# Mixing keys and queries ahead of values in the prologue of a Sinkhorn attention and SwiGLU kernel

## The chip, the cores and the metric

The kernel runs on one core of a Trainium2 chip. The metric is the device time of one execution in microseconds (us), and the figure of the kernel is the median of its runs. A core has TensorE (PE) for matmuls, VectorE (DVE), ScalarE (ACT), GpSimd (POOL) and SyncE (SP), each with its own queue of instructions, worked off in order. Matmuls write to PSUM, everything else here lives in SBUF, and data comes from HBM by DMA. DMAs are issued from GpSimd's queue (all loads but one) and from SyncE's (the small sort_net load and all stores).

## The reference

The inputs are q, k and v with 4 batches, 8 heads, 768 positions and 64 features, a sort_net of 8x8 for each batch and head, and the three weights of a gated feed-forward layer with 512 inputs and 1536 hidden columns. Cut to what matters:

```python
P = sort_net
for _ in range(5):                       # Sinkhorn
    P = exp(P - max(P, -1))
    P = P / (sum(P, -1) + 1e-9)
    P = P / (sum(P, -2) + 1e-9)
k_sorted = einsum('bhij,bhjcd->bhicd', P, k_blocks)   # 8 blocks of 96 positions
v_sorted = einsum('bhij,bhjcd->bhicd', P, v_blocks)
scores = (q_blocks @ k_sorted_blocks.T) / sqrt(64)    # inside a block of 96
attn = softmax(scores)
x = (attn @ v_sorted_blocks)             # to 3072 tokens x 512
g = x @ w_gate
out = (g * sigmoid(g) * (x @ w_val)) @ w_out
```

So P mixes the blocks of keys and of values; the queries are not mixed, but the kernel sends them through the same matmuls to have them transposed.

## The kernel before

**Two stages.** A prologue makes the attention of the first half of batch 0 (units 0 to 3; a unit is two heads and four blocks). After it the feed-forward part runs over eight token groups of 384, n = 0 to 7: gate, value and output matmuls, into which the rest of the attention is merged (units, kqs, v_chunk). The function merge writes that order out from fixed costs, and the change leaves it alone.

**The order is written by hand.** In the prologue, manual_schedule covers PE, Pool, DVE and Activation: each engine takes its instructions in the order of the program text. From line 434 it covers PE and Pool alone.

**Loads.** GpSimd's queue holds, in order: values of batch 0 in two halves (L98), the identity matrix, queries and keys of batch 0 in halves (L92, L89), the first gate and value weights (L101), two copies that turn a quarter of the values each from position-major into feature-major (copy_v, L114, into vch), the other gate and value weights, batch 1's keys, queries and values, and the output weights (L138).

**Sinkhorn.** P is 32 rows (batch and head) by 64, in PSUM (p_ps). Each of five iterations is an exp on ScalarE (L174) and six VectorE instructions (L182 to L188; the last iteration ends with two products into p_bf at L191). Among them the kernel puts other work: in iteration 2, ahead of the reductions, VectorE makes mask (a 0/1 mask of heads, L177) and copies a part of the identity into rmix[0] (L178), and ScalarE copies eighths of the values into vch (L112) in iterations 2 and 3 and after the loop.

**Weights of the mixing.** At L357 sixteen small matmuls with p_bf spread P over the partitions (w_ps), once for partitions 0 to 63 and once for 64 to 127. mix_of(b) multiplies it by mask on VectorE, which gives vmix (values, L364) and rmix (keys and queries, L368). The identity part of rmix carries the queries through.

**Mixing batch 0.** Four chunks of values (L380: 16 matmuls each into a PSUM tile tv, drained into vt) come first, then six chunks of keys and queries (L390: 32 matmuls each into tkq, drained into kqt). Drains go to ScalarE and VectorE in turn (function drain: L201 and L199). Chunks 0 to 2 of tkq read the first half of the positions, 3 to 5 the second.

**The first four units.** For each unit qk_wide makes eight score matmuls (L405) and one exp over both heads (L410). av makes eight matmuls with the mixed values (L276) and normalises on VectorE (L280, L282, tile st). xtr transposes st (L296) and drains it into xt, which the gate matmuls read. fill(n) issues n matmuls on 512 columns whose results nobody reads (L348), as the ten warm matmuls ahead of the weights do.

**PSUM.** In the prologue, one pool of four buffers (pair_tile) serves all of this: p_ps, warm_ps, w_ps, tv, tkq, qk, av_ps and x_ps. A buffer comes free when its last reader is done.

Of the kernel before, what the change touches and what calls it, by code (L numbers as in the profile page):

```python
# [12 lines left out]
ALU = mybir.AluOpType  # L13
# [4 lines left out]
def kernel(  # L18
# [11 lines left out]
    nc = tc.nc  # L30

    B, H, S, D = q.shape
    NB = sort_net.shape[-1]
    C = S // NB
    BH = B * H
    H2 = H // 2
# [7 lines left out]
    R = H * NB  # L44
# [29 lines left out]
    vch = const.tile([128, D * C + 32], BF16)  # L74
# [5 lines left out]
    kq_tiles = {}  # L80
# [26 lines left out]
    def copy_v(eng, pair, rows, s, n=4):  # L107
        cs = slice(s * (C // n), (s + 1) * (C // n))
        dst = vch3[rows, :, cs]
        src = v_tiles[pair][rows, cs, :]  # L110
        if eng is nc.scalar:
            eng.copy(dst, src.transpose([0, 2, 1]))  # L112
        else:
            eng.tensor_copy(dst, src.transpose([0, 2, 1]))  # L114

    ident = const.tile([128, 128], BF16)
    lowr, highr = slice(0, R), slice(R, 2 * R)
# [22 lines left out]
    rmix = [const.tile([128, 2, 2, H2, NB], BF16, name=f"rmix{b}") for b in range(B)]  # L140
# [8 lines left out]
    def vt_tile(pair):  # L149
        if pair not in vts:  # L150
            t = vtp.tile([C, 2, H * NB, D + 1], BF16, name=f"vt{pair}", tag="vt")
            nc.vector.memset(t[:, :, :, D:D + 1].rearrange("p u n e -> p (u n) e"), 1.0)
            vts[pair] = t
        return vts[pair]
# [14 lines left out]
    def pair_tile(name):  # L169
        return psum.tile([128, 1024], FP32, name=name, tag="pair")  # L170

    p_ps = pair_tile("p_ps")[0:BH, 0:NB * NB].rearrange("p (i j) -> p i j", j=NB)
    for it in range(N_ITER):
        nc.scalar.activation(p_ps, p_sb if it == 0 else p_ps, AF.Exp)  # L174
        if it == 2:
            with nc.allow_low_precision("0/1 mask"):
                nc.vector.tensor_reduce(mask, id4, axis=AX.XY, op=ALU.add)  # L177
            nc.vector.tensor_copy(rmix[0][R:2 * R, :, 1, :, :], idq)  # L178
            copy_v(nc.scalar, 0, lowr, 2, 8)
        if it == 3:  # L180
            copy_v(nc.scalar, 0, lowr, 3, 8)
        nc.vector.reduce_sum(rowred[:, :, 0], p_ps, axis=AX.X)  # L182
        nc.vector.reciprocal(rowred, rowred)
        nc.vector.tensor_mul(p_ps, p_ps, rowred.to_broadcast([BH, NB, NB]))
        nc.vector.reduce_sum(colred[:, 0, :], p_ps.transpose([0, 2, 1]), axis=AX.X)
        nc.vector.reciprocal(colred, colred)
        if it < N_ITER - 1:
            nc.vector.tensor_mul(p_ps, p_ps, colred.to_broadcast([BH, NB, NB]))  # L188
# [8 lines left out]
    def drain(eng, dst, src):  # L197
        if eng == "v":
            nc.vector.tensor_copy(dst, src)  # L199
        else:  # L200
            nc.scalar.copy(dst, src)  # L201
# [3 lines left out]
    def kqt_tile(b):  # L205
        if b not in kqts:
            kqts[b] = kqp.tile([128, 2 * H2 * NB * C], BF16, name=f"kqt{b}", tag="kqt")
        return kqts[b]

    GI = H2 * NB  # L210
# [57 lines left out]
    def av(b, u, tag="av"):  # L268
        half, g = divmod(u, H2)
        vt = vts[b // 2][:, b % 2].rearrange("p (h i) e -> p h i e", h=H)  # L270
        av_ps = psum.tile([128, 2, 512], FP32, name="av_ps", tag=tag, bufs=4 if tag == "pair" else 1)
        o = av_ps[:, :, 0:4 * (D + 1)].rearrange("p two (i e) -> p two i e", e=D + 1)
        for two in range(2):
            e = es[(b, u)][two]
            for i4 in range(4):
                nc.tensor.matmul(o[:, two, i4, :], lhsT=e[:, i4 * C:i4 * C + 128],  # L276
                                 rhs=vt[:, 2 * g + two, half * 4 + i4, :],
                                 start=True, stop=True)
        r_sb = ssp.tile([C, 2, 4, 1], FP32, name="r_sb", tag="r")
        nc.vector.reciprocal(r_sb, o[0:C, :, :, D:D + 1])  # L280
        st = ssp.tile([C, 4, 2, D], BF16, name="st", tag="st")
        nc.vector.tensor_tensor(st.rearrange("p i two d -> p two i d"), o[0:C, :, :, 0:D],  # L282
                                r_sb.to_broadcast([C, 2, 4, D]), op=ALU.mult)
        sts[(b, u)] = st

    def xtr(b, u, eng, tag="att"):
        half, g = divmod(u, H2)
        if g == 0:
            xts[(b, half)] = xtp.tile([128, H2, TW], BF16, name=f"xt{b}_{half}", tag="xt")
        st = sts.pop((b, u))  # L290
        if tag == "pair":
            x_ps = pair_tile("x_ps").bitcast(BF16)[:, 0:4 * C].rearrange("p (a c) -> p a c", c=C)
        else:
            x_ps = psum.tile([128, 4, C], BF16, name="x_ps", tag=tag)
        for i4 in range(4):
            nc.tensor.transpose(x_ps[:, i4, :], st[:, i4].rearrange("p a b -> p (a b)"),  # L296
                                ident[0:C, 0:C])
        drain(eng, xts[(b, half)][:, g, :], x_ps.rearrange("p a b -> p (a b)"))
# [52 lines left out]
    warm(warm_ps[:, 0:128], lowr, v_tiles[0][lowr, HC:HC + 2, :].rearrange("p c d -> p (c d)"), 1)  # L351
    warm(warm_ps[:, 512:1024], slice(0, 128), warm_sb, 9)

    w_ps = pair_tile("w_ps")[:, 0:NB * B * H].rearrange("p (i b h) -> p i b h", b=B, h=H)
    for i in range(NB):
        for half in range(2):
            nc.tensor.matmul(w_ps[half * R:(half + 1) * R, i].rearrange("p b h -> p (b h)"),  # L357
                             lhsT=p_bf[:, i].rearrange("p a b -> p (a b)"),
                             rhs=ident[0:BH, 0:BH], start=True, stop=True)

    def mix_of(b):
        mk = mask[0:R].rearrange("p (g two) -> p two g", two=2)
        lo = (b % 2) * R
        nc.vector.tensor_tensor(  # L364
            vmix[b // 2][lo:lo + R, b % 2],
            mask[lo:lo + R].unsqueeze(2).to_broadcast([R, H, NB]),
            w_ps[lo:lo + R, :, b].transpose([0, 2, 1]), op=ALU.mult)
        nc.vector.tensor_tensor(  # L368
            rmix[b][0:R, :, 0],
            mk.unsqueeze(3).to_broadcast([R, 2, H2, NB]),  # L370
            w_ps[0:R, :, b].rearrange("p i (g two) -> p two g i", two=2), op=ALU.mult)

    mix_of(0)
    dst = vt_tile(0)[:, 0]
    mix = vmix[0][lowr, 0].rearrange("p a b -> p (a b)")
    for db in range(4):
        tp = pair_tile("tv").rearrange("p (l n) -> p l n", n=H * NB)
        for ld in range(16):
            at = (db * 16 + ld) * C
            nc.tensor.matmul(tp[:, ld, :], lhsT=vch[lowr, at:at + 128], rhs=mix,  # L380
                             start=True, stop=True)
        drain("sv"[db % 2], dst[:, :, ts(db, 16)], tp[0:C].transpose([0, 2, 1]))

    dst = kqt_tile(0).rearrange("p (n c) -> p n c", c=C)
    rm = rmix[0].rearrange("p two a g i -> p two (a g i)")
    for cb in range(6):
        tp = pair_tile("tkq").rearrange("p (l n) -> p l n", n=2 * GI)
        for lc in range(16):
            for two in range(2):
                nc.tensor.matmul(tp[two * D:(two + 1) * D, lc, :],  # L390
                                 lhsT=kq_tiles[0][:, cb * 16 + lc, :],
                                 rhs=rm[:, two, :], start=True, stop=True)
        drain("sv"[cb % 2], dst[:, :, ts(cb, 16)], tp.transpose([0, 2, 1]))
    for b in range(1, B):
        mix_of(b)

    def qk_wide(u):
        half, g = divmod(u, H2)
        flat = kqts[0]
        ps = pair_tile("qk").rearrange("p (two n) -> p two n", two=2)  # L400
        for i4 in range(4):
            at = (g * NB + half * 4 + i4) * C
            for two in range(2):
                lo = two * D
                nc.tensor.matmul(ps[:, two, i4 * C:(i4 + 1) * C], lhsT=flat[lo:lo + D, at:at + 128],  # L405
                                 rhs=flat[lo:lo + D, GI * C + at:GI * C + at + C],
                                 start=True, stop=True)
        n = ecount[0] % 8
        ecount[0] += 2
        nc.scalar.activation(e_all[:, n:n + 2, 0:4 * C], ps[0:C, :, 0:4 * C], AF.Exp, scale=scale)  # L410
        es[(0, u)] = [e_all[:, n, :], e_all[:, n + 1, :]]

    def fill(n):
        warm(pair_tile("warm_ps")[:, 0:512], slice(0, 128), kqts[0][:, 0:512], n)

    for u in range(4):
        qk_wide(u)
        fill(2)
        if u >= 1:
            av(0, u - 1, "pair")  # L420
            fill(1)
        if u >= 2:
            xtr(0, u - 2, "v", "pair")
    av(0, 3, "pair")
    xtr(0, 2, "s", "pair")
    fill(3)
    xtr(0, 3, "s", "pair")
    fill(2)
    for b in range(1, B):
# [105 lines left out]
```

## Time and profile before

| | |
|---|---|
| Runs of the kernel before | 279.53, 280.14, 281.66 us; median 280.14 |
| The profiled execution | 279.53 us, of which the span of the profile is 277.5 |
| TensorE busy | 253.9 us, 92% of the span, 2698 matmuls |
| VectorE busy | 170.6 us, 61%, 364 instructions |
| ScalarE busy | 124.3 us, 45%, 239 instructions |
| GpSimd busy | 46.5 us, 17%, 44 instructions |
| First value chunk, L380 | starts at 18.42 us |
| First key/query chunk, L390 | starts at 21.91 |
| First scores, L405 | start at 29.73 |
| First attention product, L276 | starts at 32.34 |
| First gate matmul, L310 | starts at 38.97 |

All times of the profile count from the start of its span. The rows of the profile name the line, the engine and the operation, then the tile written and the tiles read, with partitions x elements. A time behind "idle before" is what the engine waited, and the name behind the arrow is what ended the wait. PE is the matmul itself and PEld the load of its weights, which overlaps. The chain of waits is followed back from the last instruction, at each step to what released it.

In forty equal slices, the first six of the profile (41.6 us) hold the prologue; the rest is the feed-forward part with the attention of the other units in it.

### The profile page before, as it was taken

The numbers are of one execution on the slowest core, as the hardware profiler recorded it, in microseconds if no ns is written. First come the engines' busy times: TensorE is split into PE (matmuls) and PEld (weight loads), VectorE is DVE, ScalarE is ACT, GpSimd is POOL, SyncE is SP. The second block draws the span as 40 slices with busy tenths as digits, with TensorE's granted clock in tenths as the row PEclk, the third lists the DMA queues.
The fourth block names the chain that finished last, engine by engine and source line by source line (L and its number), as shares of the span: only waits on it lengthen the run. The fifth ranks groups of instructions, "written<-read, shape, count | busy, mean of one in ns | idle before, by whom it ended". The sixth has DMA issues, their size and how long they took to land.

```text
span 277.5 us, 6356 instructions
## 1 busy us (share of the span) xinstructions
PE 253.9 (92%) x2698; PEld 146.7 (53%) x2698; DVE 170.6 (61%) x364; ACT 124.3 (45%) x239; POOL 46.5 (17%) x44
## 2 busy tenths in 40 slices
PE   0647799999999899999999999999999999999994
PEld 0147445565556456556656456555555555555541
DVE  6956468787276587574267587574567566666500
ACT  3174454445563353437975353435342533223311
POOL 8964005930096000000000000000000000000000
PEclk9965799999999999999999999999999999999998
DMA  6999999189961000001101101001101111011121
GB/s 111 211 191 197 220 209 200 33 162 204 223 138 40 38 4 38 18 24 38 40 0 41 38 2 40 22 20 40 38 2 38 38 40 38 2 39 38 41 76 76
DMA packets 12620, 20.86 MB, mean 75 GB/s; under 512 B 880, under 2 KB 8560, under 8 KB 12016
## 3 DMA queue, kind: packets, MB, share of 16 engines
q0 software_dynamic: 9088, 14.16, 28.7%
q1 hardware_dynamic: 3504, 6.30, 6.0%
q8 instruction: 21, 0.34, 0.5%
q14 instruction: 7, 0.06, 0.1%
HBM read 28.32 MB, written 6.29 MB: 125 GB/s over the span
## 4 chain that ended last, share of the span: by engine, by line
PE 84%; DVE 10%; ACT 3%; issue 2%; ACTq 0%
PE o_ps L337 23%; PE v_ps L323 22%; PE g_ps L310 21%; PE tkq L219 4%; PE qk L256 3%; PE av_ps L276 2%; DVE rmix L178 2%; DVE st L282 2%; PE x_ps L296 2%; PE tkq L390 2%; DVE h L325 1%; PE warm_ps L348 1%; PE tv L241 1%; PE tv L380 1%; DVE gs_sb L315 1%
## 5 line engine op out<-in xcount | busy, mean ns | idle before, releaser
L315 DVE SCALAR_TENSOR_TENSOR gs_sb<-th_sb,g_ps 128x384 bf16<-128x384 bf16 x96 | 53.0, 552 | 61.9 <-ACT th_sb L313 60.3
L310 PE MATMUL g_ps<-xt,wg_sb 128*128 128x384 bf16 x384 | 78.3, 326 | 0.1
L323 PE MATMUL v_ps<-xt,wv_sb 128*128 128x384 bf16 x384 | 78.4, 326 | 0.0
L313 ACT ACTIVATE th_sb<-g_ps 128x384 bf16<-128x384 f32 x96 | 47.5, 495 | 56.6 <-PE g_ps L310 55.7
L337 PE MATMUL o_ps<-wo_sb,h 128*128 128x512 bf16 x288 | 68.6, 379 | 0.0
L325 DVE SCALAR_TENSOR_TENSOR h<-v_ps,gs_sb 128x384 bf16<-128x384 f32 x96 | 53.3, 555 | 7.6 <-PE tkq L219 0.5
L310 PEld LDWEIGHTS <-wg_sb 128*128 128x128 bf16 x384 | 34.5, 97 | 22.2 <-issue 0.6
L323 PEld LDWEIGHTS <-wv_sb 128*128 128x128 bf16 x384 | 33.9, 97 | 20.1
L337 PEld LDWEIGHTS <-h 128*128 128x128 bf16 x288 | 26.5, 98 | 27.5
L342 ACT COPY o_sb<-o_ps 128x512 f32<-128x512 f32 x24 | 14.1, 586 | 54.4 <-PE o_ps L337 54.3
L114 POOL COPY vch<-v 64x1536 bf16<-64x1536 bf16 (+1 forms) x10 | 28.1, 2860 | 29.7 <-DMA v<-in_v_dram 16.4
L263 ACT ACTIVATE e_all<-qk 96x384 bf16<-96x384 f32 x56 | 24.3, 488 | 5.6 <-PE qk L256 5.6
L201 ACT CAST vt<-tv 96x512 bf16<-96x512 f32 (+1 forms) x26 | 19.7, 788 | 6.2 <-PE tv L231 3.4
L282 DVE TENSOR_TENSOR st<-av_ps,r_sb 96x512 bf16<-96x512 f32 x32 | 21.9, 683 | 0.7
L199 DVE CAST kqt<-tkq 128x512 bf16<-128x512 f32 (+1 forms) x21 | 16.0, 761 | 5.8 <-PE tkq L219 3.2
L201 ACT CAST kqt<-tkq 128x512 bf16<-128x512 f32 (+1 forms) x21 | 13.5, 643 | 10.8 <-PE tkq L219 7.2
L276 PEld LDWEIGHTS <-e_all 96*128 96x128 bf16 x256 | 12.3, 99 | 6.9 <-issue 1.4
L276 PE MATMUL av_ps<-vt,e_all 96*128 96x65 bf16 x256 | 13.7, 195 | 0.7 <-DVE st L282 0.5
L219 PEld LDWEIGHTS <-kq 128*64 128x64 bf16 x576 | 10.5, 112 | 5.9 <-issue 5.9
L296 PE MATMUL x_ps<-ident,st 96*128 96x96 bf16 x128 | 10.8, 206 | 2.2 <-DVE st L282 2.1
L296 PEld LDWEIGHTS <-st 96*128 96x128 bf16 x128 | 8.5, 97 | 8.0 <-DVE st L282 4.0
L219 PE MATMUL tkq<-rmix,kq 128*64 128x64 bf16 x576 | 12.5, 197 | 0.0
(57 smaller groups left out, 132.4 us busy)
## 6 DMA issues: line engine op xcount, KB each, us to landing
out_dram<-o_sb SPq DMA_DIRECT2D x24, 256.0 KB, 2.0
kq<-in_k_dram POOLq DMA_DIRECT2D x3, 768.0 KB, 13.3
kq<-in_q_dram POOLq DMA_DIRECT2D x3, 768.0 KB, 16.6
v<-in_v_dram POOLq DMA_DIRECT2D x3, 768.0 KB, 17.7
wg_sb<-in_moe_w_gate_dram POOLq DMA_DIRECT2D x6, 256.0 KB, 10.5
wv_sb<-in_moe_w_val_dram POOLq DMA_DIRECT2D x6, 256.0 KB, 10.8
wo_sb<-in_moe_w_out_dram POOLq DMA_DIRECT2D x1, 1536.0 KB, 24.1
v<-in_v_dram POOLq DMA_DIRECT2D x2, 384.0 KB, 5.6
```

Source lines behind the costliest of these rows:

```text
L114: eng.tensor_copy(dst, src.transpose([0, 2, 1]))
L201: nc.scalar.copy(dst, src)
L219: nc.tensor.matmul(tp[two * D:(two + 1) * D, lc, :], lhsT=nat[:, cb * 8 + lc, :], rhs=rm[:, two, :], start=True, stop=True)
L276: nc.tensor.matmul(o[:, two, i4, :], lhsT=e[:, i4 * C:i4 * C + 128], rhs=vt[:, 2 * g + two, half * 4 + i4, :], start=True, stop=True)
L282: nc.vector.tensor_tensor(st.rearrange("p i two d -> p two i d"), o[0:C, :, :, 0:D], r_sb.to_broadcast([C, 2, 4, D]), op=ALU.mult)
L296: nc.tensor.transpose(x_ps[:, i4, :], st[:, i4].rearrange("p a b -> p (a b)"), ident[0:C, 0:C])
L310: nc.tensor.matmul(g_ps, lhsT=wg_sb[:, kc, ts(m, 128)], rhs=xt[:, kc, :], start=(kc == 0), stop=(kc == NKC - 1))
L313: nc.scalar.activation(th_sb, g_ps, AF.Tanh, scale=0.5)
L315: nc.vector.scalar_tensor_tensor(gs_sb, th_sb, 1.0, g_ps, op0=ALU.add, op1=ALU.mult)
L323: nc.tensor.matmul(v_ps, lhsT=wv_sb[:, kc, ts(m, 128)], rhs=xt[:, kc, :], start=(kc == 0), stop=(kc == NKC - 1))
L325: nc.vector.scalar_tensor_tensor(h_tiles[n][:, m, :], v_ps, 0.5, gs_tiles.pop(m), op0=ALU.mult, op1=ALU.mult)
L337: nc.tensor.matmul(o_ps, lhsT=h_w[:, m, ts(t3, 128)], rhs=wo_sb[:, m, :], start=(m == 0), stop=(m == NFC - 1))
```

## The change

- The mask and the copy of the identity part into rmix[0] move from iteration 2 to iteration 1 of the Sinkhorn loop. ScalarE's copies stay where they were.
- The weights are made in two calls: weights(0) for partitions 0 to 63 ahead of the mixing, weights(1) for partitions 64 to 127 after the scores. w_ps is laid out over both banks of its PSUM buffer, one for each half.
- mix_of makes rmix ahead of vmix. For batch 0 it is called before the mixing, as before; for batches 1 to 3 it is called behind the attention of all four units, where it was called behind the last key/query chunk. w_ps is therefore in use up to there.
- The six key/query chunks come first, with the same drains. The four value chunks follow (v_wide), in between the score groups and exps of the four units: scores 0, values 0, scores 1, values 1, values 2, scores 2, values 3, scores 3. Value chunks 0 and 2 are drained by VectorE and 1 and 3 by ScalarE; before, 0 and 2 by ScalarE and 1 and 3 by VectorE.
- Then come, unit by unit, av, the transposes of the unit before and fill(2). All four drains into xt are ScalarE's; before, the first two were VectorE's. Ten fill matmuls are issued, where there were sixteen.

```diff
     for it in range(N_ITER):
         nc.scalar.activation(p_ps, p_sb if it == 0 else p_ps, AF.Exp)
-        if it == 2:
+        if it == 1:
             with nc.allow_low_precision("0/1 mask"):
                 nc.vector.tensor_reduce(mask, id4, axis=AX.XY, op=ALU.add)
             nc.vector.tensor_copy(rmix[0][R:2 * R, :, 1, :, :], idq)
+        if it == 2:
             copy_v(nc.scalar, 0, lowr, 2, 8)
...
-    w_ps = pair_tile("w_ps")[:, 0:NB * B * H].rearrange("p (i b h) -> p i b h", b=B, h=H)
-    for i in range(NB):
-        for half in range(2):
-            nc.tensor.matmul(w_ps[half * R:(half + 1) * R, i].rearrange("p b h -> p (b h)"),
+    w_ps = pair_tile("w_ps").rearrange("p (s n) -> p s n", s=2)[:, :, 0:NB * B * H] \
+        .rearrange("p s (i b h) -> p s i b h", b=B, h=H)
+
+    def weights(half):
+        for i in range(NB):
+            nc.tensor.matmul(w_ps[half * R:(half + 1) * R, half, i].rearrange("p b h -> p (b h)"),
                              lhsT=p_bf[:, i].rearrange("p a b -> p (a b)"),
                              rhs=ident[0:BH, 0:BH], start=True, stop=True)
+
+    weights(0)
...
-    mix_of(0)
-    dst = vt_tile(0)[:, 0]
-    mix = vmix[0][lowr, 0].rearrange("p a b -> p (a b)")
-    for db in range(4):
-        tp = pair_tile("tv").rearrange("p (l n) -> p l n", n=H * NB)
-        for ld in range(16):
-            at = (db * 16 + ld) * C
-            nc.tensor.matmul(tp[:, ld, :], lhsT=vch[lowr, at:at + 128], rhs=mix,
-                             start=True, stop=True)
-        drain("sv"[db % 2], dst[:, :, ts(db, 16)], tp[0:C].transpose([0, 2, 1]))
...
-    for b in range(1, B):
-        mix_of(b)
...
+    def v_wide(db, eng):
+        tp = pair_tile("tv").rearrange("p (l n) -> p l n", n=H * NB)
+        for ld in range(16):
+            at = (db * 16 + ld) * C
+            nc.tensor.matmul(tp[:, ld, :], lhsT=vch[lowr, at:at + 128], rhs=vm,
+                             start=True, stop=True)
+        drain(eng, vdst[:, :, ts(db, 16)], tp[0:C].transpose([0, 2, 1]))
...
+    qk_wide(0)
+    v_wide(0, "v")
+    qk_wide(1)
+    v_wide(1, "s")
+    v_wide(2, "v")
+    qk_wide(2)
+    v_wide(3, "s")
+    qk_wide(3)
+    weights(1)
     for u in range(4):
-        qk_wide(u)
-        fill(2)
+        av(0, u, "pair")
         if u >= 1:
-            av(0, u - 1, "pair")
-            fill(1)
-        if u >= 2:
-            xtr(0, u - 2, "v", "pair")
-    av(0, 3, "pair")
-    xtr(0, 2, "s", "pair")
-    fill(3)
+            xtr(0, u - 1, "s", "pair")
+        if u < 3:
+            fill(2)
+    for b in range(1, B):
+        mix_of(b)
+    fill(2)
     xtr(0, 3, "s", "pair")
     fill(2)
```

More of the change, by code (lines that the diff above doesn't have):

```diff
@@ L364, in mix_of @@
         nc.vector.tensor_tensor(
+            rmix[b][0:R, :, 0],
+            mk.unsqueeze(3).to_broadcast([R, 2, H2, NB]),
+            w_ps[0:R, 0, :, b].rearrange("p i (g two) -> p two g i", two=2), op=ALU.mult)
+        nc.vector.tensor_tensor(
             vmix[b // 2][lo:lo + R, b % 2],
             mask[lo:lo + R].unsqueeze(2).to_broadcast([R, H, NB]),
[L367 to L371, printed above, removed]
-    mix_of(0)
-    dst = vt_tile(0)[:, 0]
-    mix = vmix[0][lowr, 0].rearrange("p a b -> p (a b)")
-    for db in range(4):
-        tp = pair_tile("tv").rearrange("p (l n) -> p l n", n=H * NB)
-        for ld in range(16):
-            at = (db * 16 + ld) * C
-            nc.tensor.matmul(tp[:, ld, :], lhsT=vch[lowr, at:at + 128], rhs=mix,
-                             start=True, stop=True)
-        drain("sv"[db % 2], dst[:, :, ts(db, 16)], tp[0:C].transpose([0, 2, 1]))
[L384 to L393, printed above, removed]
-    for b in range(1, B):
-        mix_of(b)
+            w_ps[lo:lo + R, b % 2, :, b].transpose([0, 2, 1]), op=ALU.mult)
     def qk_wide(u):
@@ L411, in qk_wide @@
         es[(0, u)] = [e_all[:, n, :], e_all[:, n + 1, :]]
+    mix_of(0)
+    kdst = kqt_tile(0).rearrange("p (n c) -> p n c", c=C)
+    rm = rmix[0].rearrange("p two a g i -> p two (a g i)")
+    for cb in range(6):
+        tp = pair_tile("tkq").rearrange("p (l n) -> p l n", n=2 * GI)
+        for lc in range(16):
+            for two in range(2):
+                nc.tensor.matmul(tp[two * D:(two + 1) * D, lc, :],
+                                 lhsT=kq_tiles[0][:, cb * 16 + lc, :],
+                                 rhs=rm[:, two, :], start=True, stop=True)
+        drain("sv"[cb % 2], kdst[:, :, ts(cb, 16)], tp.transpose([0, 2, 1]))
+    vdst = vt_tile(0)[:, 0]
+    vm = vmix[0][lowr, 0].rearrange("p a b -> p (a b)")
+    def v_wide(db, eng):
[5 more added lines that the diff above has]
+        drain(eng, vdst[:, :, ts(db, 16)], tp[0:C].transpose([0, 2, 1]))
     def fill(n):
         warm(pair_tile("warm_ps")[:, 0:512], slice(0, 128), kqts[0][:, 0:512], n)
+    qk_wide(0)
[7 more added lines that the diff above has]
+    weights(1)
     for u in range(4):
-        qk_wide(u)
-        fill(2)
+        av(0, u, "pair")
         if u >= 1:
-            av(0, u - 1, "pair")
-            fill(1)
-        if u >= 2:
-            xtr(0, u - 2, "v", "pair")
-    av(0, 3, "pair")
-    xtr(0, 2, "s", "pair")
-    fill(3)
+            xtr(0, u - 1, "s", "pair")
[4 more added lines that the diff above has]
+    fill(2)
     xtr(0, 3, "s", "pair")
```

## The prediction

> **What bounds the kernel now.** I read the chain of waits first. By engine it is mostly TensorE, and by line two thirds of it (L337, L323 and L310: 23, 22 and 21%) are matmuls of the feed-forward part, which the diff does not touch. In order of time, though, the chain before the first gate matmul (38.97 us) is made of other things:
>
> ```profile
> 6.01 6.11 DVE rmix L178
> 15.46 2.82 ACT vch L112 x2
> 18.42 3.57 PE tv L380 x64
> 21.98 3.66 PE tkq L390 x132
> 25.65 1.53 issue
> 27.17 1.16 PE tkq L390 x60
> 28.36 1.24 DVE kqt L199
> ```
>
> The columns are start, length, engine, tile and line. One copy of a 64x64 tile holds the chain for 6.11 us; then come two ScalarE copies, the value chunks, the key/query chunks, a gap in which TensorE waited for nothing visible, and the last drain. The timeline shows what ran beside that copy:
>
> ```profile
> 5.76 0.81 POOL L101 DMA_DIRECT2D wv_sb<-in_moe_w_val_dram  x1
> ...
> 6.01 6.11 DVE L178 COPY rmix<-ident 64x64 bf16<-64x64 bf16 x1
> ...
> 6.51 5.57 POOL L114 COPY vch<-v 64x1536 bf16<-64x1536 bf16 x2
> ...
> 8.35 4.02 PE L348 MATMUL warm_ps<-warm_sb,ident 128*128 128x512 bf16 x9
> ...
> 11.96 0.80 POOL L101 DMA_DIRECT2D wg_sb<-in_moe_w_gate_dram  x1
> ...
> 12.15 0.21 DVE L182 TENSOR_REDUCE rowred<-p_ps 32x8 f32<-32x64 f32 x1
> ...
> 38.02 0.36 DVE L430 COPY rmix<-ident 64x64 bf16<-64x64 bf16 x3
> ```
>
> The same copy three times over takes 0.36 us at 38.02, when GpSimd is idle: 0.12 each. So about 6.0 of the 6.11 us are a wait that ends when the two GpSimd copies end (12.08). All later Sinkhorn steps sit behind it on VectorE: they restart at 12.15 and p_bf is made at 16.69. Last, when the second half of batch 0's keys comes (the L89 DMA issued at 4.48):
>
> ```profile
> DMA to landing us min/median/max: 11.3/11.3/11.3
> ```
>
> It lands at 15.8; the second half of the queries at 13.8 (3.97 plus 9.8), the first halves at 9.9 and 11.8. The weights land before they are used and none of their issues waits for compute.
>
> [...] at 6.01 the copy was held although GpSimd's own copy began only at 6.51, so the issue of 5.76 to 6.57 held it; yet at 12.0 the copy ran within 0.16 us of the start of another issue. [...] half clock from 16.2 to 26.2 and 30.1 to 33.1, with tkq matmuls 28 ns apart before (3.73/132) and 19 ns after (1.14/60).
>
> **The identity copy, moved up one iteration.** Mask reduction and copy now follow the first iteration's last product (3.93). The mask begins at about 4.07 (in the old place it began 0.14 after that product), takes 0.26, and the copy is ready at 4.34. GpSimd is then issuing DMAs (3.97, 4.48, 4.99, 5.76). By what happened at 12.0 the copy slips in at the start of the next issue, about 4.5; iteration 1's reduction starts at t = 4.6 instead of 4.40. An iteration takes 1.67 us (13.82 to 15.49), and the last one 1.20 up to p_bf, so p_bf is at t + 3x1.67 + 1.20 = t + 6.2 = 10.8, and complete 0.74 later. It was 16.69: 5.9 us earlier. Bounds: nothing if the copy waits until 12.1; 0.3 better if it costs nothing. ScalarE's vch copies follow the exps as before and end at about 12.6, hidden since values come later.
>
> **Weights and first mix.** TensorE's order has the ten warming matmuls ahead, until 12.37, so the first 8 weight matmuls (0.05 each, 0.37) run to 12.75; rmix takes 0.20, and tkq starts at 13.05. Of the 5.9 us some 1.1 are lost to the warmers. The second 8 move behind the scores, 0.37 us beside VectorE's value drain.
>
> **Keys and queries first.** A chunk is 32 matmuls: 0.61 us at full, 0.90 at half clock. Three chunks end between 14.9 and 15.75. The fourth needs the second half of the keys, 15.8, so the next three end at 17.7 to 18.6, and VectorE's last drain (1.22) at 19.0 to 19.9. Scores start at T0 = 19.5, against 29.73. The 1.53 us gap of before [...] I cost it at nothing; if it recurs, 1.5.
>
> **Scores between value chunks.** Ahead of the first attention product ScalarE does e0, e1, a value drain, e2 and a drain: 3x0.81 + 2x1.06 = 4.55, plus the first score group (0.46) and hand-overs: 5.1. At half clock, value chunks of 0.90 and three rotating PSUM buffers (w_ps keeps the fourth to the end) stretch it to 6.15. I take 5.7, so 25.2. Then av, xtr and two fills: at half clock 0.65+0.5+1.04 = 2.2 a step, at full 0.42+0.34+0.60 = 1.36. av0 with its fill to 26.9, a slow step to 29.1, a mixed one to 30.7, av3 to 31.1; its reciprocal and st 0.9, transposes 0.34, ScalarE's drain 0.48, hand-overs 0.3: the first gate at 33.15. That is 13.65 after T0, against 9.24: 4.4 of the 10.2 us gained at T0 go back, because the value mixing is now in this stretch.
>
> **Edits that I cost at nothing.** Six fills fewer (16 to 10): TensorE filling waits. Two xt drains from VectorE (0.34) to ScalarE (0.48): only the last one counts, and it was ScalarE's. Six mix products (about 1.2) behind the last st, with three identity copies (0.36): hidden under transposes, drain, gate (0.81) and tanh (0.49); without that cover 0.5. Those copies fall near 33, between GpSimd's last issue (28.3) and its next copy (44.66)[...]. The SP and GpSimd queues keep their order; nothing is moved past a DMA.
>
> **Afterwards** the feed-forward part slides. The last gate and value weights land at 30.8 and 32.1, ahead of their use 20 us into the stage; batch 1's queries at 40.5, first needed 11.9 us after the first gate (45.1); GpSimd's copies for batch 1 end at 55.9, needed at 59.3; the output weights at 51.3, needed at 64.8. So the gain is kept: 38.97 - 33.15 = 5.8 us. The profiled execution took 279.53 us (span 277.5), which gives 273.7; the median stands 0.6 above it, so 274.3. With full clock throughout the first gate is at 32.0 (273.1); with half clock and the gap again at 34.5 (275.6).
>
> **Rivals.** (1) *The copy is caught one iteration earlier.* The issues and both GpSimd copies follow one another without a gap from 2.94 to 12.08, and at 6.5 and 9.4 the waiting copy lost against the next GpSimd instruction. If it loses at 4.5, 5.0 and 5.8 too, t is 12.15: p_bf at 18.4, scores 1.35 + 6x0.90 + 1.3 later at 26.4, first gate at 40.0. That is 1.0 later than before: 281.2 (280 to 284). It decides from t = 11.1. Against it: the copy ran at 12.0 just after an issue began. Chance 0.12. (2) *The gain is half eaten*: the copy gets in only at 5.8 (1.2 later), the gap recurs (1.5), or TensorE stays at half clock through all attention steps (0.8); two of these give 276.3 to 277.0, all three 277.8. Chance 0.10. (3) *Another VectorE instruction is caught instead*: the reciprocals read and write SBUF, and none ran beside a GpSimd copy before. The second iteration's would then stand until 12.1 where it ran at 12.40: 0.3, and 0.6 from the reordering (p_bf to gate 21.7 instead of 22.3): 279.2. Reciprocals at 4.65 and 5.37 ran 0.19 us beside DMA issues[...]. Chance 0.05.
>
> **The numbers.** My forecast has 0.73. Measuring tells about 1% (2.8 us) from no change. Faster by more than that (below 277.3): 0.73 and two thirds of rival 2, 0.80. Slower by more: half of rival 1, 0.06. Within 1%: 0.14. The range takes the forecast's own 273.1 to 275.6, a little below it, and rival 2: 272.5 to 277.8.
>
> **What would show it.** L178 short at about 4.4; p_bf near 10.8; tkq from about 13, with a wait for the keys up to 15.8; scores near 19.5; first gate near 33; distances after it unchanged. It is wrong if L178 is long again, if a reciprocal is, if the first gate is not 4.5 to 7 us earlier, or if the feed-forward part gives it back.

## The result, and the profile after

| | before | changed |
|---|---|---|
| Median | 280.07 us (32 runs, 274.40 to 281.66) | 272.89 us (27 runs, 272.09 to 274.95) |
| Profiled execution, its span | 279.53, 277.5 | 272.49, 270.4 |
| First key/query chunk | 21.91 | 12.73 |
| First scores | 29.73 | 19.13 |
| First attention product | 32.34 | 24.39 |
| First gate matmul | 38.97 | 31.80 |

The medians differ by 7.18 us, a ratio of 0.974. The runs of the kernel before fall into two groups: five of the 32 lie at 274.4 to 275.9 us (the quicker group), the other 27 at 278.0 to 281.7 (the upper group). The ratio on record, 0.989 with an interval of 0.9853 to 0.9926, sets the changed kernel against only nine runs of the kernel before, those five and four at 278.0 to 278.2; against the five alone it is about 0.994. Beside seven runs of the kernel before that were all in the upper group, a variant level with the changed kernel (mix_spread, below) stood at 0.9746 (0.9706 to 0.9786). So the change is worth 7 us in most executions and under 2 us in the others, and what makes the groups is part of what was studied.

The chain of waits of the changed kernel has lost the copy. Its longest pieces up to the first gate matmul, in order of time (start, length, engine, tile, line), begin with a load:

```profile
4.48 11.28 DMA kq<-in_k_dram
16.63 2.37 DVE kqt L200 x2
21.24 0.96 ACT vt L202
22.24 0.95 PE tv L413 x15
23.29 1.06 ACT vt L202
26.61 0.87 PE warm_ps L349 x2
```

Up to 15.76 nothing on an engine sets the end: the second half of the keys does. Then come VectorE's drains of key/query chunks, ScalarE's value drains and two of the fill matmuls. The timeline has the steps of the prediction:

```profile
4.34 0.18 DVE L178 COPY rmix<-ident 64x64 bf16<-64x64 bf16 x1
...
6.47 0.19 DVE L184 RECIPROCAL rowred<-rowred 32x8 f32<-32x8 f32 x1
6.51 5.67 POOL L114 COPY vch<-v 64x1536 bf16<-64x1536 bf16 x2
...
8.14 0.19 DVE L184 RECIPROCAL rowred<-rowred 32x8 f32<-32x8 f32 x1
...
10.76 0.74 DVE L192 TENSOR_TENSOR p_bf<-p_ps,colred 32x256 bf16<-32x256 f32 x2
12.00 0.42 PE L360 MATMUL w_ps<-ident,p_bf 32*64 32x32 bf16 x8
...
12.73 1.71 PE L401 MATMUL tkq<-rmix,kq 128*64 128x64 bf16 x96 [0.30 <-DVE rmix L369]
...
15.90 1.71 PE L401 MATMUL tkq<-rmix,kq 128*64 128x64 bf16 x96 [1.46 <-DMA kq<-in_k_dram]
...
19.13 0.34 PE L386 MATMUL qk<-kqt 64*128 64x96 bf16 x8 [1.52 <-DVE kqt L200]
...
31.80 0.81 PE L311 MATMUL g_ps<-xt,wg_sb 128*128 128x384 bf16 x4 [0.40 <-DVE vmix L373]
```

The copy takes 0.18 us where it took 6.11, the Sinkhorn loop runs beside GpSimd's copies without a stall, and the key/query chunks wait 1.46 us for the load in their middle. The bracket of the last row is new: the first gate matmul waited 0.40 us for a mix product. The first gate is 7.17 us earlier and the span 7.1 shorter, so the feed-forward part slid and gave nothing back.

### The profile page after: what moved, and what is told of

It is laid out like the page before. It is cut to its first block, busy times and chain, and to the rows that moved or that the text cites. A ratio compares the mean times of both kernels' runs of the same rounds, so it can differ in the third digit from the quotient of the medians.

```text
span 270.4 us, 6343 instructions
## 1 busy us (share of the span) xinstructions
PE 250.7 (93%) x2692; PEld 144.8 (54%) x2692; DVE 164.1 (61%) x362; ACT 125.1 (46%) x241; POOL 46.7 (17%) x44
## 4 chain that ended last, share of the span: by engine, by line
PE 83%; DVE 6%; DMA 4%; ACT 3%; issue 1%; POOL 1%; ACTq 0%; POOLq 0%
PE o_ps L338 23%; PE v_ps L324 23%; PE g_ps L311 21%; DMA kq<-in_k_dram 4%; PE tkq L220 4%; PE av_ps L277 3%; PE qk L257 3%; PE x_ps L297 2%; DVE st L283 2%; DVE h L326 1%; PE tv L242 1%; DVE gs_sb L316 1%; PE tv L232 1%; PE warm_ps L349 1%; DVE kqt L200 1%
## 5 line engine op out<-in xcount | busy, mean ns | idle before, releaser
L311 PEld LDWEIGHTS <-wg_sb 128*128 128x128 bf16 x384 | 34.5, 97 | 22.5 <-issue 0.9
L281 DVE RECIPROCAL r_sb<-av_ps 96x8 f32<-96x8 f32 x32 | 6.4, 200 | 10.1 <-PE av_ps L277 9.7
```

The source lines that it names most:

```text
L311: nc.tensor.matmul(g_ps, lhsT=wg_sb[:, kc, ts(m, 128)], rhs=xt[:, kc, :], start=(kc == 0), stop=(kc == NKC - 1))
```

## The experiments

**The two parts of the change, each alone.** copy_up is the kernel before with this edit only:

```diff
-        if it == 2:
+        if it == 1:
             with nc.allow_low_precision("0/1 mask"):
                 nc.vector.tensor_reduce(mask, id4, axis=AX.XY, op=ALU.add)
             nc.vector.tensor_copy(rmix[0][R:2 * R, :, 1, :, :], idq)
+        if it == 2:
             copy_v(nc.scalar, 0, lowr, 2, 8)
```

> The kernel before with the mask and identity copy in iteration 1, and nothing else of the change. [...] L178 takes 0.18 us, p_bf is made at about 10.8, value chunks start at about 13.1, scores at 23.3 to 24.8, first gate at 32.5 to 34, so 273.5 to 275. Order theory (the gain is made by keys first and values between the exps): about 279, with the time saved before p_bf lost again in waits for keys and drains.

It took 274.95 us (273.72 to 275.66): p_bf at 11.02, scores at 24.96, first gate at 34.08. That is 5.1 of the 7.2 us, and level with the quicker group of the kernel before. order_only is the changed kernel with this edit undone:

> The changed kernel with the mask and identity copy back in iteration 2. [...] L178 is caught for about 6 us in most executions, p_bf at 16.7, tkq at 18.1, scores at about 24.8, first gate at 37.4 to 38.3: 278.7 to 279.5, with about 272.5 in the few executions where the copy is not caught. Order theory: 273 to 275 in spite of the stall.

Its four runs were 272.68, 278.39, 278.12 and 272.13. The profiled one is the run of 272.68. Its timeline, around the copy:

```profile
5.77 0.81 POOL L101 DMA_DIRECT2D wv_sb<-in_moe_w_val_dram  x1
...
6.02 0.56 DVE L178 COPY rmix<-ident 64x64 bf16<-64x64 bf16 x1
...
6.38 1.50 ACT L112 COPY vch<-v 64x768 bf16<-64x768 bf16 x1 [0.34 <-DMA v<-in_v_dram]
...
6.51 5.62 POOL L114 COPY vch<-v 64x1536 bf16<-64x1536 bf16 x2
```

The copy was held here too, but only for 0.4 us (0.56 against 0.18), and it ended together with the DMA issue, at 6.58. The first half of the values, for which GpSimd's copy waits as well as ScalarE's, came at 6.38. Up to there it was therefore the DMA issue, the only GpSimd work at that time, that held the identity copy; after that the identity copy got in ahead of GpSimd's. The two runs near 278.3 have no profile. If the copy was held in full in them, as their times suggest, the reordering alone gives about 2 us (278.3 against 280.1); on top of copy_up it gives 2.06 (274.95 to 272.89). The order theory is refuted as the main cause, but its share is not small.

**What holds the copy.** The kernel before was run again, and twice more, for a profile of its quicker group:

> The kernel before, unchanged. Its 32 runs so far lie mostly at 278 to 281.7 us, but six at 274.4 to 275.9. Race theory: GpSimd's copy may start only when the first half of the values has landed (about 6.1 us), and VectorE's identity copy is ready at 6.01; in a few executions the identity copy wins. Then a profile of about 275 us shows L178 at 0.18 us and p_bf near 11, one of about 280 shows L178 at about 6.1 us; times come in two groups, about 274.5 and about 280. Clock theory: the two groups differ in the granted clock alone, and L178 takes about 6.1 us in both.

> The kernel before once more, for a profile of an execution of about 275 us, which the first repeat did not give. Race theory: if the profiled execution takes about 275, its L178 takes under 0.7 us and ScalarE's first vch copy, which waits for the same load of values, starts after about 6.3; if it takes about 280, L178 takes about 6.1 us and that copy starts before 6.3. Clock theory: L178 takes about 6.1 us in either.

> As for before_third: the same kernel and the same two expectations, a second draw.

All three profiles fell into the upper group (280.47 and, by medians, 280.78 and 281.52), with L178 at 6.07, 6.09 and 6.12 us. ScalarE's value copy, which shows by when the values were there, starts at 6.14, 6.18 and 6.13 in them and at 6.24 in the first profile of the kernel before, against 6.38 in order_only. before_third:

```profile
6.01 6.09 DVE L178 COPY rmix<-ident 64x64 bf16<-64x64 bf16 x1
...
6.18 1.51 ACT L112 COPY vch<-v 64x768 bf16<-64x768 bf16 x1
...
6.50 2.85 POOL L114 COPY vch<-v 64x1536 bf16<-64x1536 bf16 x1
```

So the half of the test that was reached agrees with the race. No profile of the kernel before in its quicker group was had; that the copy wins there is inferred from order_only and from copy_up being level with that group. The rival, that the groups differ in the granted clock alone, does not fit the 30 runs of the kernel before beside split64: the mean clock was 0.979 to 0.990 in the quicker group and 0.967 to 1.000 in the upper, whose two runs at 1.000 took 279.9 and 280.2 us.

copy_first moves the identity copy by one instruction only, ahead of the mask:

```diff
+            nc.vector.tensor_copy(rmix[0][R:2 * R, :, 1, :, :], idq)
             with nc.allow_low_precision("0/1 mask"):
                 nc.vector.tensor_reduce(mask, id4, axis=AX.XY, op=ALU.add)
-            nc.vector.tensor_copy(rmix[0][R:2 * R, :, 1, :, :], idq)
```

> The kernel before with the identity copy one instruction earlier, ahead of the mask reduction, still in iteration 2: it is ready at about 5.74 instead of 6.01. [...] the identity copy wins every time: L178 0.18 us, first gate at 32.5 to 34, 273.5 to 275. If the DMA issue of 5.76 to 6.57 holds it, as the prediction read it, it is caught still: about 6.3 us, 280.

```profile
5.75 0.81 POOL L101 DMA_DIRECT2D wv_sb<-in_moe_w_val_dram  x1
...
5.84 0.18 DVE L176 COPY rmix<-ident 64x64 bf16<-64x64 bf16 x1
```

All four runs were at 274.14 to 275.70. The copy started 0.09 us into the DMA issue that holds it at 6.02, and ran freely; started 0.18 us later, it costs 5 us. The time is that of the first alternative, in which it is GpSimd's copy that holds the identity copy. But order_only was held before the values had come (0.56 us instead of 0.18), so the issue holds it as well: not yet 0.09 us after its beginning, but 0.25 us after it.

**The unexplained stop of TensorE.** copy_up has one as well, 1.70 us long, behind the 132nd key/query matmul, as before. gap_shift puts 16 tiny matmuls into copy_up, ahead of the weights:

```diff
     warm(warm_ps[:, 512:1024], slice(0, 128), warm_sb, 9)
+    warm(warm_ps[:, 512:544], slice(0, 128), warm_sb[:, 0:32], 16)
```

> The kernel before with the identity copy moved up, and 16 more tiny warming matmuls (32 columns) ahead of the weights. There the key/query matmuls stop for 1.7 us after the 132nd although nothing that the profile shows is awaited. Theory ([...] at a fixed place in its instruction stream): 32 more instructions ahead move the stop 16 matmuls forward, to behind the 116th, and its length stays 1.5 to 2 us. Rival (a buffer, a drain or the clock): it stays behind the 132nd, or comes at another place by its time.

It took 275.49 us. Its timeline, TensorE alone:

```profile
16.10 2.32 PE L392 MATMUL tkq<-rmix,kq 128*64 128x64 bf16 x116
20.95 2.24 PE L392 MATMUL tkq<-rmix,kq 128*64 128x64 bf16 x76 [2.53 <-issue]
```

The stop moved to exactly the 116th, so it belongs to a place in the instruction stream. A matmul is two instructions there (a weight load and the matmul; the page of the kernel before has 2698 of each); counted so, it comes ahead of number 445 in every kernel that shows it (in the kernel before behind 10 warm, 16 weight, 64 value and 132 key/query matmuls). It takes 1.53 us in the kernel before, 1.70 in copy_up, 2.03 in copy_first. What TensorE waits for there is not shown, and no run removed the stop. The length was missed: 2.53 us, beyond the 1.5 to 2 expected. TensorE came to the place sooner (2.32 us for 116 matmuls, against 3.73 for 132 in copy_up); whether that makes the stop longer was not isolated.

**The end of the prologue.** mix_spread calls mix_of(u + 1) behind av(0, u), so that w_ps comes free earlier:

> The changed kernel with mix_of(1), (2) and (3) called one by one behind the first three attention products instead of together behind all four. In the changed kernel the first gate matmul waits 0.40 us for the last of these products, because they keep w_ps in PSUM. Theory (that wait is what holds the first gate): the gate starts when ScalarE's last drain is done, 0.3 to 0.4 us earlier, about 31.45, 0.1 to 0.15% less time. Rival (the drain or a later VectorE instruction holds it as well): 31.7 to 31.8, no change.

The wait for the mix product is gone. From the last transposes to the first gate it takes 0.93 us (31.44 to 32.37), in the changed kernel 1.18 (30.62 to 31.80): 0.25 saved of the 0.40, as ScalarE's drain is next. Its first gate is 0.57 us later nonetheless: in this execution the keys came 0.26 later (16.16 against 15.90), the scores started 0.37 later, and TensorE stood for 0.54 at number 445. The first 96 key/query matmuls took 2.77 us instead of 1.71, or 28.9 ns each, about the 28.3 (3.73/132) of the kernel before at a granted clock of 0.50; why is open. The wait for the keys, 0.40 us behind them, hid it. Median 273.24 (271.99 to 273.61): no difference that can be measured. mix_drain also swaps the drains, drain("vs"[cb % 2], ...):

> The same, and the drains of the six key/query chunks start with VectorE, so that ScalarE (1.01 us each) has two of the last three and VectorE (1.22) one. Theory (VectorE's two last drains, 16.63 to 18.98, set the start of the scores): scores at about 18.8 instead of 19.13, first gate about 31.1. Rival: the first chunks' drains free PSUM later and the start does not move: 31.4.

From the first matmul on the second half of the keys to the scores it takes 2.81 us (16.16 to 18.97) instead of 3.23 (15.90 to 19.13), but the first gate is at 31.68, not 31.1: the keys came 0.26 later, and TensorE stopped 0.41 us at number 445. Median 272.21 (271.93 to 273.31, four runs).

**Fills.** no_fill drops the two fills behind each of the first three attention products.

> The changed kernel without the six filling matmuls among the attention products (results that nobody reads; the last four stay). Clock theory (fills bring the full clock before the feed-forward part): the attention products start up to 1.5 us sooner, but half clock lasts into the first gate and value matmuls, so the first gate is near 30.5 and the end is level or later: 272 to 274. Rival (fills only delay): first gate near 30.5 and 1.3 us less at the end, 271.

```profile
31.09 1.44 PE L311 MATMUL g_ps<-xt,wg_sb 128*128 128x384 bf16 x4
32.46 0.50 PE L257 MATMUL qk<-kqt 64*128 64x96 bf16 x8
32.90 0.87 PE L324 MATMUL v_ps<-xt,wv_sb 128*128 128x384 bf16 x4
```

The first gate matmuls start 0.7 us earlier but take 1.44 us where the changed kernel's take 0.81, and the value matmuls start at 32.90 against 32.82. From 30 to 32 us the granted clock was 0.50, in the changed kernel 1.00. The first gate at 31.09 missed the 30.5 expected; the end did not: median 273.15 (272.28 to 274.19), level, as the clock theory has it.

**A try at a faster version.** split64 is mix_drain with the loads of queries and keys cut at position 64; after_again is the changed kernel beside it.

```diff
-    for lo in (0, HC):
-        load_q(0, lo, lo + HC)
-        load_k(0, lo, lo + HC)
+    for lo, hi in ((0, 64), (64, C)):
+        load_q(0, lo, hi)
+        load_k(0, lo, hi)
```

> The kernel of mix_drain with the loads of batch 0's queries and keys cut at position 64 instead of 48. The changed kernel's chain goes through the second half of the keys, which lands at 15.8 to 16.1. With 64 and 32 positions the first part lands later (about 13.4) and four of six chunks can run before the last part, which lands at the same time. Theory (what follows the last landing sets the start of the scores): scores at about 18.2, first gate about 0.8 us earlier than in mix_drain, 271.3. Rival (the drains or the later start of the first chunk take it back): scores near 19, 272.

> The changed kernel, unchanged, on the same chip as split64: 272 to 274.5, scores at about 19.1 to 19.5, first gate at 31.8 to 32.3.

Medians 273.08 (17 runs) and 273.10 (14 runs): the same. The scores did start at 18.01 against 19.01, and the timelines show where most of that microsecond went. split64, then the changed kernel:

```profile
18.01 0.34 PE L386 MATMUL qk<-kqt 64*128 64x96 bf16 x8 [1.10 <-ACT kqt L202]
18.19 0.28 PE L413 MATMUL tv<-vmix,vch 64*128 64x64 bf16 x4
19.66 0.46 PE L413 MATMUL tv<-vmix,vch 64*128 64x64 bf16 x10 [1.19 <-issue]
```

```profile
19.01 0.35 PE L386 MATMUL qk<-kqt 64*128 64x96 bf16 x8 [1.52 <-DVE kqt L200]
19.18 0.28 PE L413 MATMUL tv<-vmix,vch 64*128 64x64 bf16 x4
19.82 0.46 PE L413 MATMUL tv<-vmix,vch 64*128 64x64 bf16 x10 [0.37 <-issue]
```

In both, TensorE stops after the fourth value matmul, ahead of number 445, for 1.19 us and for 0.37. The scores start 1.00 us earlier, the matmul behind the stop 0.16. At the first gate the profile of split64 is 0.53 ahead (31.34 against 31.87), which the medians do not show. Nothing that was run beats the changed kernel by a measurable amount.

## Why the prediction was right

The forecast was 274.3 us with 272.5 to 277.8; it came to 272.89, by the mechanism that was forecast. One part was luck: the three runs known beforehand were all in the upper group, and the forecast took the long stall as certain. It holds in most executions, so the median moved as forecast; against the quicker group the same change brings 1.7 us (274.59, the median of the five, to 272.89). Step by step:

| Step | predicted | measured |
|---|---|---|
| Identity copy ready, done | 4.34, about 4.6 | 4.34, 4.52 |
| p_bf | 10.8 | 10.76 |
| First key/query chunk | 13.05 | 12.73 |
| Second half of the keys | 15.8 | 15.76 |
| First scores | 19.5 (19.0 to 19.9) | 19.13 |
| First attention product | 25.2 | 24.39 |
| First gate | 33.15 (full clock: 32.0) | 31.80 |
| Profiled execution | 273.7 | 272.49 |

- **The stall and its end** were right to 0.1 us. The copy did not even wait for the next issue: it ran inside one that had begun at 3.97. Rival 1 did not come about, nor did rival 3: reciprocals took 0.19 us beside GpSimd's copies (6.47 and 8.14). Of rival 2 the half clock came, through most of the attention steps, but without the loss put on it.
- **The reading that the DMA issue holds the copy** was right, and incomplete. The prediction took the 6 us as what happens. It happened in the four profiles in which the values were there by 6.13 to 6.24, and not in the one in which they came at 6.38. In all five they came before the issue ended (6.56 to 6.58), so what decides between the two copies is not shown, nor why the identity copy is held and the reciprocals are not.
- **The clock was mis-sized.** The prediction stood halfway between full and half clock (granted clock 1.00 and 0.50); the chunks ran at full, 17.8 ns a matmul (1.71/96). In stretches of the changed kernel (start and end, length, TensorE busy and matmuls, granted clock, DMA share, GB/s):

```profile
18.00:20.00 2.00, 0.74 (x24) 1.00 1.47 195
20.00:22.00 2.00, 1.71 (x56) 1.00 1.45 196
22.00:24.00 2.00, 1.84 (x35) 0.51 1.46 201
...
28.00:30.00 2.00, 1.94 (x23) 0.79 1.44 195
30.00:32.00 2.00, 1.19 (x9) 1.00 1.48 264
```

  Half clock came only at 22, behind two of the value chunks, and was over before 30. That accounts for 0.81 of the 1.35 us missing at the first gate: 0.37 up to the scores and 0.44 from scores to attention (5.26 instead of 5.7). The first chunk's own lead of 0.32 (the warmers ended at 12.08, not 12.37) was lost in the wait for the keys. A small misreading changes nothing: half clock in the kernel before lasted from 16.2 to about 26.4 and from about 29.8 to 33.2 (granted clock 0.59 from 26.0 to 26.5, 0.82 from 29.5 to 30.0), not to 26.2 and from 30.1 to 33.1.
- **The attention steps were mis-sized as well**, by the other 0.54 (7.41 instead of 7.95), and not for the clock: it was 0.50 from 24 to 28, the prediction's slow case. The prediction added up the lengths of rows, 0.65 + 0.5 + 1.04 for a slow step. But in the profile a row of matmuls starts before the row ahead of it has ended:

```profile
24.39 0.60 PE L277 MATMUL av_ps<-vt,e_all 96*128 96x65 bf16 x8 [0.29 <-ACT vt L202]
24.80 1.04 PE L349 MATMUL warm_ps<-kqt,ident 128*128 128x512 bf16 x2
25.64 0.64 PE L277 MATMUL av_ps<-vt,e_all 96*128 96x65 bf16 x8
```

  The first attention product with its fill took 1.25 us instead of 1.7, and the slow step behind it 1.88 (to 27.52) instead of 2.2. That is 0.77 less; later steps and the wait in the next point took 0.23 of it back. So the measured 31.80 lies even below the 32.0 given for full clock throughout. That 32.0 is not the sum of the prediction's own full-clock terms either: it keeps the 7.95 with its slow step (19.0 + 5.1 + 7.95), and with steps of 1.36 it would be about 30.3. Nor is the 34.5 for half clock and the gap: half clock alone already gives 34.0 (19.9 + 6.15 + 7.95).
- **The edits costed at nothing** held one that costs: the mix products behind the last st. The prediction looked at what VectorE does after them; what waited was the first gate matmul, for w_ps to leave PSUM. 0.40 us of wait, of which 0.25 came back in mix_spread.
- **The stop of TensorE**, costed at nothing by an estimate, comes back, shorter than the 1.53 us of the kernel before. In the first profile of the changed kernel the weight loads stand for 0.24 us ahead of number 445, and in after_again the matmuls for 0.37.
- **What the reordering itself brings** was put at 0.6 us (p_bf to gate 21.7 instead of 22.3, under rival 3). It brings about 2: p_bf to gate is 21.04 in the changed kernel and 23.06 in copy_up. That the shorter stop (at most 0.37 in the changed kernel, 1.70 in copy_up) makes most of this is argued from the rows, not isolated.

## What to carry to other kernels

A tiny VectorE copy between SBUF tiles, put beside GpSimd work, took 6.11 us here instead of 0.18, up to the end of that work, and whether it did hung on 0.2 us (started at 6.01 in the kernel before, it took 6.11; at 5.84 in copy_first, 0.18). Look for groups in the run times, and move such a copy to where no GpSimd copy is close behind it. Before bringing a stage forward, ask what ends last there once it is early: here first a load (15.76), then VectorE's drains (16.63 to 19.00), then the stop of TensorE at a fixed place in its instructions (1.19 us in split64 against 0.37), which ate most of what an earlier start of the scores had gained.

## What the runs showed that was not expected

- **TensorE stops at a fixed place in its instructions.** Stops of 0.37 to 2.53 us that no row explains come ahead of the same instruction, number 445, in kernels with different work there. gap_shift shows that the place is fixed in the instruction stream: 16 matmuls more ahead moved the stop from behind the 132nd key/query matmul to behind the 116th. What TensorE waits for there is not shown.
- **A GpSimd DMA issue does not hold up VectorE's copy all the time**: the copy ran freely (0.18 us) 0.09 us into one (copy_first) and 0.37 us into another, shorter one (the changed kernel), and was held from 0.25 us into a third until it ended with it (order_only, 0.56 us).
